# A windowed-attention and softplus feed-forward kernel: value products token by token in the scores' tile shape, softmax division on ScalarE, and visits at written times

## The chip, the cores and the metric

One core of one Trainium2 chip runs the whole program in one launch. The metric is the device time of that launch in microseconds (us), over several runs; beside it stands one execution taken by the hardware profiler, whose rows are quoted below. The engines are PE (TensorE; PEld are its weight loads), DVE (VectorE), ACT (ScalarE), POOL (GpSimd) and SP, which issues nearly all DMAs.

## What is computed

Attention of 8 heads over 4608 tokens (8 sequences of 576), head size 64, where each query sees 32 keys: the last 32 positions in heads 0 to 3, every fourth of the last 128 in heads 4 to 7. Its output, 512 features per token, goes through a feed-forward layer with softplus between its two matrices. All of it is fp32.

```python
scores = scale * np.matmul(q, k.transpose(0, 1, 3, 2))
scores = np.where(masks[None, :, :, :], scores, -1000000000.0)
attn = np.exp(scores - np.max(scores, axis=-1, keepdims=True))
attn = attn / (np.sum(attn, axis=-1, keepdims=True) + 1e-09)
x = np.matmul(attn, v)            # then tokens x 512 features
h = x @ w_in                      # 512 x 2048
g = np.maximum(h, 0.0) + np.log1p(np.exp(-np.abs(h)))
return (g @ w_out).astype(np.float32)
```

## The kernel before

**Tokens** are cut into 9 chunks of 512. A chunk's attention is four **groups** (class `Group`, L368), 36 in all; the groups of chunks 0 and 1 are called early here, those of chunks 2 to 8 late (28 of them). A group is two heads times 512 tokens: groups 0 and 1 of a chunk are the plain heads, 2 and 3 the strided ones.

**A late group** runs so: 32 small matmuls give the scores (`score`, L403: 64 contraction rows, 32 queries, 64 keys, so the array is cut into tiles of 64 rows by 32 columns). DVE scales and masks them out of PSUM (L445) and takes the maximum (L456); ACT takes eight exponentials of 64 columns each with their sums (L467); DVE takes the reciprocal of the sums (L479, L482), divides (`divide`, L485) and transposes squares of 32x32 (L507); the squares go to DRAM ("turned") and come back as `pt` with keys on the partitions (`send_squares`, `fetch_squares`). Then 32 small matmuls give the values (`weighted`, L543): the stationary operand is v (64 keys by 64 features), the moving one the weights of 32 queries, so the tiles are 64x64. The result stands feature by feature, and ACT copies it as it is out of PSUM into `x_full` (`x_high`, L592, L596), which is one kt quarter of the 512 features. Scores of one group and values of an earlier one share the bank pair `sv_ps`, each in one half of a bank.

**The feed-forward** multiplies in two or three parts (a high and a low part of each fp32 operand, tiles named `xh`/`xl`, `g` and `parts`). Chunks 0 to 2 go through it in 48 slots (`h_part` L660, `o_part` L709: each 12 matmuls of 128x512). Chunks 3 to 8 go in three pairs, each as seven products of blocks in place of eight (names a11 to s4 and t1 to t4); `prepared` (L1371) builds the sums and splits of the blocks of x from `x_full`, `product` gives h, `block_step` the output.

**What sets the order.** Up to slot 9 the order is written out by hand in `OPENING`; a word is an action and its number (S scores, M maximum, E exponentials, Pv divide, T transposes, C copy, V values, Xh and Xl the two parts of x, D decode a weight, H, G, O the feed-forward). Slots 10 to 21 follow a loop with fixed moments (`attend`, L953, for groups 8 to 11). From slot 22 on a planner writes the program: every piece of work is a `Task` with an engine, a cost and what it waits for; DVE, ACT, POOL and SP take the open task of lowest rank, PE takes from two queues of feed-forward work and from the list of **visits** (`choose`, L1898). A visit is the scores of group n, with the values of an earlier group right behind them where these are ready (`together`; for n below 20 the group before, from then on two before). A visit is due 12 or 16 us after the last (`VISIT_EVERY`, `LATE_VISITS`). The order that comes out is kept as written on each engine. All matmuls stand at L242, all DMAs of SP at L177.

Of the kernel before, what the change touches and what calls it, by code (L numbers as in the profile page):

```python
# [24 lines left out]
P = 128  # L25
# [11 lines left out]
PKW = CH + WIN  # L37
DKW = DIL * (CH // DIL + WIN)
SW = NS * WKEYS
# [15 lines left out]
PREPARED_SOONER = -3.0  # L55
# [4 lines left out]
FAMILY_SOONER = 5.0  # L60
LATE_VISITS = 16.0
# [9 lines left out]
HANDED_VISIT = 2.0  # L71
MARGIN = 0.4
VISIT_EVERY = 12.0
# [25 lines left out]
v0 S4 Dl1_0 M4 k5 C0 q5 r3 E2 T1 V0 C1 D0_0_1 v1 Pv3 Z2 Pv2 T2 D1_0_1 Xh0 v2 Xl0 E4 C2 D2_0_1 D3_0_1  # L99
D0_2_0 v3 r4 S5 M5 D4_0_1 Z4 H1_0 E5 r5 D1_2_0 D2_2_0 D3_2_0 k6 q6 H0_0 Pv4 T3 V1 r6 v4 Xh1 C3 D5_0_1 V2  # L100
Xh2 Xl1 T4 Z5 Xl2 C4 V3 r7 Xh3 D4_2_0 k7 v5 Pv5 H1_1 H1_2 D0_1_1 Xl3 H0_1 D5_2_0 D1_1_1 H1_3 D0_3_0
Dl0_1 A1 Dl2_0 H0_2 H0_3 S6 D1_3_0 D2_3_0 A0 D3_3_0 T5 C5 G1 H2_0 D2_1_1 D3_1_1 D4_3_0 D5_3_0 H2_1 G0
H2_2 H2_3 M6 Dl3_0 Gs1 Gs0 Gl0 V4 H3_0 H3_1 H3_2 D0_4_0 D0_2_1 D1_2_1 D2_2_1 Xh4 D4_1_1 Xl4 H3_3 O0_0 E6
Gl1 Z6 D5_1_1 D3_2_1 D4_2_1 Dl1_1 D1_4_0 D2_4_0 A2 O0_1 O0_2 G2 V5 Xh5 Xl5 D3_4_0 D4_4_0 A3 G3 D5_4_0
Dl4_0 O0_3 Gs2 Gl2 O1_0 O1_1 O1_2 q7 r8 D0_3_1 r9 S7 O1_3 r10 M7 r11 v6 r12 v7 D0_4_1 D5_2_1 Dl2_1 Pv6
H4_0 H4_1 H5_0 H5_1 H4_2 E7 H4_3 r13 D1_3_1 O2_0 O2_1 r14 A4 T6 D1_4_1 D2_4_1 C6 O2_2 V6 D3_4_1 Z7
D2_3_1 D3_3_1 D4_3_1 D0_5_0 G4 Pv7 O2_3 H6_0 H6_1 D5_3_1 Xh6 Gs3 Xl6 D4_4_1 D1_5_0 r15 T7 r16 m2 r17 q8
r18 H5_2 H6_2 Dl3_1 D2_5_0 Gl3 C7 Gs4 V7 r19 D0_7_0 D5_4_1 O3_0 O3_1 D1_7_0 Dl4_1 Xh7 Xl7 Gl4 H5_3
D0_6_1 O3_2 H6_3 D1_6_1 D3_5_0 D2_6_1 A5 O3_3 O4_0 O4_1 D4_5_0 D5_5_0 G5 O4_2 H7_0 D2_7_0 A6 Dl5_0
D3_7_0 D3_6_1 K0 D0_6_0 Gs5 r20 G6 H7_1 O4_3 D1_6_0 D4_6_1 H7_2 H8_0 H8_1 H8_2 D4_7_0 Gl5 D5_6_1 r21 k8  # L110
v8 r22 Gs6 D5_7_0 K1 Dl6_1 D2_6_0 Dl7_0 r23 D0_8_0 K2 D0_5_1 K3 H8_3 H7_3 O5_0 D3_6_0 Gl6 D1_8_0 O5_1
D1_5_1 D4_6_0 O5_2 r24 O5_3 A7 D5_6_0 A8 r25 D2_8_0 D2_5_1 G7 r26 r27 r28 O6_0 O6_1 O6_2 H9_0 H9_1 Gs7
H9_2 D3_5_1 D3_8_0 H9_3 D4_5_1 D4_8_0 D5_5_1 D5_8_0 Gl7 O6_3 G8 A9 O7_0 O7_1 r29 r30 Gs8 Dl8_0 Dl5_1 G9
O7_2 Gl8 Dl6_0 O7_3 Gs9 r31 Gl9
# [4 lines left out]
def tile_windowed_attention_softplus_ffn(  # L119
# [4 lines left out]
    kdl: bass.AP,  # L124
    vp: bass.AP,
# [160 lines left out]
    def load_mask(c):  # L286
# [6 lines left out]
        load_dma(out=masks[c], in_=cst[c, :, P:] if c < FIRST else msk[c])  # L293
# [42 lines left out]
    WHOLE = slice(0, 2)  # L336

    def combine(d, name, kt=WHOLE):

# [5 lines left out]
            out=raw_block(d, name)[:, kt], in0=raw_block(d, a)[:, kt], in1=raw_block(d, b)[:, kt], op=op  # L345
        ))

    def split_high(d, name, kt=WHOLE):
# [4 lines left out]
        pin(nc.scalar.copy(out=blocks[name][0][:, kt], in_=raw_block(d, name)[:, kt]))  # L353

    def split_low(d, name, kt=WHOLE):
        high, low = blocks[name]
        pin(nc.vector.tensor_tensor(
            out=low[:, kt], in0=raw_block(d, name)[:, kt], in1=high[:, kt].bitcast(F32), op=ALU.subtract
        ))

    def first_of(dil, t, g):

        t2, h = divmod(t, 2)
        if dil:
            return g * PER + (2 * h + t2) * BLK, g * (PER + WIN) + (2 * h + t2) * BLK
        return ((h * 2 + t2) * NG + g) * BLK, ((h * 2 + t2) * NG + g) * BLK
# [1688 lines left out]
```

## Time and profile before

| | before |
|---|---|
| median of 3 runs | 826.92 us (825.87 to 827.13) |
| profiled execution, first to last instruction | 827.4 us |
| PE busy | 813.3 us, 98% |
| DVE busy | 654.0 us, 79% |
| ACT busy | 579.0 us, 70% |
| POOL busy | 65.0 us, 8% |
| DMA | 194.81 MB, mean 235 GB/s |

The runs are whole executions; the profile is one execution with its rows counted from the first to the last instruction, 0.5 us above the median. In the rows, "x64" is a count of instructions put together, "[1.17 <-DVE s]" an idle time and what ended it. A fp32 matmul of the small shapes leaves two records, so the 32 matmuls of a group are x64. A record's own length is longer than the distance from one start to the next, since matmuls overlap; it is the starts that tell the pace.

### The profile page before, as it was taken

The numbers are of one execution on the slowest core, as the hardware profiler recorded it, in microseconds if no ns is written. First come the engines' busy times: TensorE is split into PE (matmuls) and PEld (weight loads), VectorE is DVE, ScalarE is ACT, GpSimd is POOL, SyncE is SP. The second block draws the span as 40 slices with busy tenths as digits, with TensorE's granted clock in tenths as the row PEclk, the third lists the DMA queues.
The fourth block names the chain that finished last, engine by engine and source line by source line (L and its number), as shares of the span: only waits on it lengthen the run. The fifth ranks groups of instructions, "written<-read, shape, count | busy, mean of one in ns | idle before, by whom it ended". The sixth has DMA issues, their size and how long they took to land.

```text
span 827.4 us, 19611 instructions
## 1 busy us (share of the span) xinstructions
PE 813.3 (98%) x7861; PEld 663.0 (80%) x7861; DVE 654.0 (79%) x936; ACT 579.0 (70%) x1241; POOL 65.0 (8%) x74
## 2 busy tenths in 40 slices
PE   7899999999999999999999999999999999999998
PEld 3778888888888888888888888888778887888886
DVE  5798899957797788787889886978899757577964
ACT  6898778757676877588878637788696345776732
POOL 0000000031354360000000000000000000000000
PEclk9899999999999999999999999999999999999999
DMA  8895934468999887756677878888766576666652
GB/s 285 290 315 179 323 95 144 135 206 281 299 311 349 302 313 239 226 147 196 219 256 256 300 238 274 296 281 268 238 208 205 190 243 203 191 203 210 221 194 88
DMA packets 102778, 194.81 MB, mean 235 GB/s; under 512 B 9248, under 2 KB 49568, under 8 KB 102688
## 3 DMA queue, kind: packets, MB, share of 16 engines
q1 hardware_dynamic: 102544, 193.29, 71.3%
q8 instruction: 62, 1.02, 0.5%
q10 hardware_dynamic: 144, 0.28, 0.1%
q14 instruction: 28, 0.23, 0.1%
HBM read 145.29 MB, written 48.23 MB: 234 GB/s over the span
## 4 chain that ended last, share of the span: by engine, by line
PE 90%; DMA 9%; ACT 0%; DVE 0%; issue 0%; DVEq 0%; SPq 0%
PE o_ps L242 43%; PE h_ps L242 14%; PE h_x L242 13%; PE h_y L242 13%; PE sv_ps L242 6%; DMA raw<-w 3%; DMA v<-vp 3%; DMA k<-kpl 1%; DMA t<-w_o 1%; DMA turned<-squares 1%; DMA pt<-turned 1%; PE a_ps L242 0%; DVE g L1499 0%; ACT g L1495 0%; ACT pt L534 0%
## 5 line engine op out<-in xcount | busy, mean ns | idle before, releaser
L242 PE MATMUL o_ps<-g,t 128*128 128x512 f32 x867 | 208.1, 389 | 0.7 <-DMA t<-w_o 0.7
L242 PEld LDWEIGHTS o_ps<-g,t 128*128 128x128 f32 x867 | 162.1, 188 | 34.8 <-DMA t<-w_o 1.2
L242 PE MATMUL o_ps<-g,parts 128*128 128x512 f32 x576 | 142.3, 392 | 0.0
L242 PE MATMUL h_ps<-xh,parts 128*128 128x512 f32 x384 | 130.2, 397 | 0.0
L242 PEld LDWEIGHTS o_ps<-g,parts 128*128 128x128 f32 x576 | 107.2, 188 | 22.4
L1495 ACT CAST g<-stored 128x1024 fp32r<-128x1024 f32 x72 | 75.5, 1050 | 66.2 <-PE o_ps L242 63.0
L1499 DVE TENSOR_TENSOR g<-stored,g 128x1024 fp32r<-128x1024 f32 x72 | 87.8, 1221 | 32.4 <-ACT g L1495 32.1
L242 PEld LDWEIGHTS h_ps<-xh,parts 128*128 128x128 f32 x384 | 72.6, 189 | 15.7
L467 ACT ACTIVATE s<-s,nm 128x64 f32<-128x64 f32 x224 | 74.9, 337 | 8.3 <-DVE nm L456 8.0
L242 PE MATMUL h_ps<-xl,parts 128*128 128x512 f32 x192 | 75.3, 392 | 0.0
L242 PE MATMUL h_x<-s,t 128*128 128x512 f32 x276 | 70.5, 391 | 0.0
L242 PE MATMUL h_y<-s,t 128*128 128x512 f32 x276 | 70.4, 390 | 0.0
L818 POOL TENSOR_TENSOR a<-a 128x256 f32<-128x256 f32 x64 | 59.1, 929 | 99.0 <-DVE a L813 86.9
L242 PEld LDWEIGHTS h_y<-s,t 128*128 128x128 f32 x276 | 51.6, 188 | 10.9
L1475 DVE SCALAR_TENSOR_TENSOR stored<-stored,e 128x1024 f32<-128x1024 f32 x48 | 58.3, 1218 | 2.5 <-ACT e L1471 2.5
L242 PEld LDWEIGHTS h_x<-s,t 128*128 128x128 f32 x276 | 51.6, 188 | 10.8
L1490 DVE TENSOR_TENSOR stored<-stored 128x1024 f32<-128x1024 f32 x48 | 58.3, 1219 | 0.4
L682 DVE SCALAR_TENSOR_TENSOR e<-h_ps,e 128x512 f32<-128x512 f32 x48 | 32.8, 683 | 25.2 <-ACT e L1170 20.5
L1465 ACT ACTIVATE e<-stored 128x1024 f32<-128x1024 f32 x48 | 50.4, 1054 | 2.4 <-DVE stored L1454 1.2
L1471 ACT ACTIVATE e<-e 128x1024 f32<-128x1024 f32 x48 | 50.8, 1060 | 1.0
L1468 ACT ACTIVATE e<-e 128x1024 f32<-128x1024 f32 x48 | 50.7, 1057 | 0.9
L467 ACT ACTIVATION_READ_ACCUMULATOR s<-s,nm 128x1 f32 x224 | 42.3, 189 | 0.0
(104 smaller groups left out, 1244.4 us busy)
## 6 DMA issues: line engine op xcount, KB each, us to landing
t<-w_o SPq DMA_DIRECT2D x84, 512.0 KB, 4.2
raw<-w SPq DMA_DIRECT2D x64, 256.0 KB, 5.2
v<-vp SPq DMA_DIRECT2D x28, 512.0 KB, 5.2
t<-w SPq DMA_DIRECT2D x20, 512.0 KB, 4.0
t<-w_two SPq DMA_DIRECT2D x20, 512.0 KB, 4.4
q<-qp SPq DMA_DIRECT2D x35, 256.0 KB, 3.7
w_o<-stage SPq DMA_DIRECT2D x32, 256.0 KB, 3.9
t<-w_one SPq DMA_DIRECT2D x16, 512.0 KB, 4.7
```

Source lines behind the costliest of these rows:

```text
L242: return tc.keep_in_program_order(nc.tensor.matmul(**kw))
L467: pin(nc.scalar.activation(out=self.blocks[:, t], in_=src, func=AF.Exp, bias=self.nm[:, t : t + 1], scale=1.0 / 8.0 if self.masked else 1. ...
L682: pin(nc.vector.scalar_tensor_tensor(out=e, in0=tiles.pop(i), scalar=0.0, in1=e, op0=ALU.max, op1=ALU.add))
L818: pin(nc.gpsimd.tensor_tensor(out=out, in0=in0, in1=in1, op=ALU.subtract))
L1465: pin(nc.scalar.activation(out=es[key], in_=raw_g(*key), func=AF.Abs))
L1468: pin(nc.scalar.activation(out=es[key], in_=es[key], func=AF.Exp, scale=-1.0))
L1471: pin(nc.scalar.activation(out=es[key], in_=es[key], func=AF.Ln, bias=1.0))
L1475: pin(nc.vector.scalar_tensor_tensor(out=h, in0=h, scalar=0.0, in1=es.pop(key), op0=ALU.max, op1=ALU.add))
L1490: pin(nc.vector.tensor_tensor(out=raw_g(c, *PLACE[name]), in0=raw_g(c, *PLACE[a]), in1=raw_g(c, *PLACE[b]), op=op))
L1495: pin(nc.scalar.copy(out=set_of(k)[0], in_=raw_g(c, *PLACE[name])))
L1499: pin(nc.vector.tensor_tensor(out=low, in0=raw_g(c, *PLACE[name]), in1=high.bitcast(F32), op=ALU.subtract))
```

## The change

**Late groups** hold four heads times 256 tokens in place of two heads times 512 (two groups for the plain heads, two for the strided). The values matmuls are swapped: the weights are stationary (64 keys by 32 queries) and v moves (64 features), so they have the scores' tile shape, 64x32, and the result stands token by token. It is not divided before: `divide` is gone for late groups, and `shares` reads the values out of PSUM with eight ACT instructions of 64 columns, each scaled by the reciprocal of its sum, back into `pt`. `unturned` then turns squares of 32x32 on DVE into `x_full` (one instruction of 512 columns for strided heads, two of 256 for plain ones). The copy L596 is gone.

**Early groups** get the same values matmuls (their division stays where it was); `unturned` turns them out of PSUM into `s`, and `x_high` and `x_low` read that and no longer PSUM. With this a kt quarter of the features of a chunk takes two groups, where before it took one.

**Loads.** A late group has its own mask (128 KB; before, one for the four groups of a chunk) and 640 columns of keys (before, 544 for plain heads).

**Order.** `VISITS_AT` gives each visit of the planner's part a written time, in place of the two spacings; the ranks of two families of tasks are moved (`FAMILY_SOONER` 5 to 13, `PREPARED_SOONER` -3 to 4); the planner's costs follow (values 1.30 to 1.00, both together 2.10 to 1.60; new: shares 1.70, unturned 0.72 or 0.84); the next `bring` waits for `unturned` of the group before and no longer for its values; `OPENING` is written anew.

```diff
-PKW = CH + WIN
+PKW = CH + 2 * WIN
+LKW = DIL * (CH // DIL + WIN)
+MW = NS // 2 * WKEYS
-PREPARED_SOONER = -3.0
+PREPARED_SOONER = 4.0
-FAMILY_SOONER = 5.0
-LATE_VISITS = 16.0
+FAMILY_SOONER = 13.0
-HANDED_VISIT = 2.0
-MARGIN = 0.4
-VISIT_EVERY = 12.0
+VISITS_AT = (
+    4, 27.5, 40, 50.5, 60, 85.5, 101, 108.5, 140, 149.5, 174, 189.5,
+    204, 211.5, 235, 250.5, 266, 281.5, 297, 304.5, 332, 343.5, 363, 378.5,
+)
+MARGIN = 0.5
...
+    def load_mask(c, pr=0):
+        if c >= FIRST:
+            masks[c, pr] = wk.tile([P, 2 * SW], BF16, name="mask", bufs=1)
+            load_dma(out=masks[c, pr], in_=msk[c - FIRST, pr])
+            return
...
         def weighted(self, shared=None, following=None):
+            if self.c >= FIRST:
+                by_block = self.v.rearrange("p i r d -> p (i r) d")
+                for m, g in itertools.product(range(NS), range(NG)):
+                    at_col = m // 2 * HALF + MW + m % 2 * D
+                    for h in range(2):
                         begun = matmul(
-                            out=dst,
-                            lhsT=self.v[h * WKEYS : (h + 1) * WKEYS, i, r, :],
-                            rhs=self.weights_of(h, r * 2 + t2, g),
+                            out=banks[h][g * SQ : (g + 1) * SQ, at_col : at_col + D],
+                            lhsT=self.weights_of(h, m, g),
+                            rhs=by_block[h * WKEYS : (h + 1) * WKEYS, m * NG + g],
...
+        def shares(self):
+            self.x = self.pt.rearrange("p g n -> p (g n)").rearrange("p (b n) -> p b n", n=D)
+            for n in range(NB):
+                m, h = n // 2, n % 2
+                at_col = m // 2 * HALF + MW + m % 2 * D
+                divided = nc.scalar.activation(
+                    out=self.x[:, n], in_=self.values_in[h][:, at_col : at_col + D], func=AF.Copy,
+                    scale=self.ri[:, n : n + 1],
+                )
+                pin(divided)
...
+        def unturned(self):
             if self.c >= FIRST:
+                by_square = self.x.rearrange("p b (d k) -> p b d k", d=2)
+                x = x_half(self.c, self.dil)
+                if self.dil:
+                    pin(nc.vector.transpose(
+                        out=x[:, :, self.j * HALF : (self.j + 1) * HALF].rearrange("p d (b q) -> p b d q", q=SQ),
+                        in_=by_square,
+                    ))
+                    return
+                for d in range(2):
+                    by_block = x[:, d].rearrange("p (c b q) -> p b c q", c=DIL, q=BLK // DIL)
+                    pin(nc.vector.transpose(
+                        out=by_block[:, self.j * NB : (self.j + 1) * NB],
+                        in_=by_square[:, :, d].rearrange("p b (c q) -> p b c q", c=DIL),
+                    ))
                 return
...
         def x_high(self):
-            for dh, _, src in self.x_parts():
-                copied = nc.scalar.copy(out=dh, in_=src)
-                pin(copied)
+            high, x = self.x_part(0)
+            pin(nc.scalar.copy(out=high, in_=x))
...
     def values_of(n):
-        v = valued[n] = Task(f"values {n}", PE, 1.30, lambda: value_of(n), deps)
+        v = valued[n] = Task(f"values {n}", PE, 1.00, lambda: value_of(n), deps)
+        shares = Task(f"shares {n}", ACT, 1.70, groups[n].shares, [v, scaled_of.get(partner(n)), divided_of.get(n)], rank=0.3)
         x_done[n] = Task(
-            f"x {n}", ACT, 0.60, groups[n].x_high, [v, scaled_of.get(partner(n)), *x_uses.get(n // 2, [])], rank=0.3
+            f"unturned {n}", DVE, 0.72 if groups[n].dil else 0.84, groups[n].unturned,
+            [shares, *x_uses.get(n // 2, [])], rank=0.3,
         )
...
-        last = Task(f"divide {n}", DVE, 0.70, lambda: g.divide(nc.vector), [last], rank=0.3)
-        brought[n] = Task(f"bring {n}", SP, 0.5, g.fetch_squares, [last, Later(lambda: valued.get(n - 1))], rank=0.1)
+        brought[n] = Task(f"bring {n}", SP, 0.5, g.fetch_squares, [last, Later(lambda: x_done.get(n - 1))], rank=0.1)
...
-        together[scored[n]] = Task(f"both {n}", PE, 2.10, both)
-    spaced, done_second = HANDED_VISIT, 0
+        together[scored[n]] = Task(f"both {n}", PE, 1.60, both)
...
-            if t >= spaced and visits[0].open(t) and (urgent or visits[1] in scores or joins(visits[1], t)):
+            visit_at = VISITS_AT[len(VISITS_AT) - sum(v in scores for v in visits)]
+            if t >= visit_at and visits[0].open(t) and (urgent or visits[1] in scores or joins(visits[1], t)):
                 return visits
...
-                spaced = t + (VISIT_EVERY if len(visits) > 32 else LATE_VISITS)
```

**Where the order moves.** PE, the visit with the scores of the last group (`sv_ps<-k,q`), before:

```order
L242 MATMUL h_y<-s_4335,t 128x512 x4
L242 MATMUL h_y<-s_4336,t 128x512 x2
L242 MATMUL sv_ps<-k,q 32x64 x32
L242 MATMUL sv_ps<-pt,v 64x4x8 x32
L242 MATMUL h_x<-a_4374,t 128x512 x4
L242 MATMUL h_x<-a_4375,t 128x512 x2
```

and of the change:

```order
L246 MATMUL h_x<-s_4564,t 128x512 x4
L246 MATMUL h_x<-s_4565,t 128x512 x2
L246 MATMUL sv_ps<-k,q 32x64 x32
L246 MATMUL sv_ps<-v,pt 32x64 x32
L246 MATMUL h_y<-a_3909,t 128x512 x4
L246 MATMUL h_y<-a_3910,t 128x512 x2
```

The same two pieces stand side by side; the values (`sv_ps<-..` the second row) have the scores' shape 32x64 now. Over the whole planner's part and the loop ahead of it, 21 of the 28 late groups had their values right behind scores; of the change it is 19. The last two groups' values, which stood 54 and 84 matmuls of 128x512 behind this visit, stand 48 and 174 behind it.

PE in the opening (`t_ps` transposes of the weights, `a_ps` values of an early group, `s_ps` scores), before:

```order
L496 MATMUL t_ps<-ident,s 128x128 x4
L242 MATMUL a_ps<-pt,v 64x4x8 x32
L496 MATMUL t_ps<-ident,s 128x128 x4
L242 MATMUL s_ps<-k,q 32x64 x32
L242 LDWEIGHTS consts
L242 MATMUL s_ps<-mask,consts 128x256
```

and of the change:

```order
L517 MATMUL t_ps<-ident,s 128x128 x4
L246 MATMUL a_ps<-v,pt 32x2x32 x32
L517 MATMUL t_ps<-ident,s 128x128 x4
L246 MATMUL a_ps<-v,pt 32x2x32 x32
L246 MATMUL s_ps<-k,q 32x64 x32
L246 LDWEIGHTS consts
```

The values of group 1 now stand ahead of the scores of group 5; before, they stood behind these and the first six matmuls of the feed-forward.

ACT near that last visit (`s,sm<-s,nm` exponentials, `e` softplus), before:

```order
L1471 ACTIVATE e<-e 128x1024
L467 ACTIVATE s,sm<-s,nm 128x64 x5
L596 COPY x_full<-sv_ps 128x512
L1495 CAST g<-stored 128x1024
L1452 COPY temps<-h_y 128x512
L353 CAST a_3928<-x_full 128x1024
```

and of the change:

```order
L1547 ACTIVATE e<-e 128x1024
L1550 ACTIVATE e<-e 128x1024
L1531 COPY temps<-h_y 128x512
L623 ACTIVATE pt<-sv_ps,ri 128x64 x8
L488 ACTIVATE s,sm<-s,nm 128x64 x3
L1531 COPY stored<-h_y 128x512
```

One copy `x_full<-sv_ps` is replaced by eight instructions `pt<-sv_ps,ri`; here they stand ahead of the last group's exponentials, where the copy stood behind them.

## Rows read from the trace of the kernel before

**Rows 1.** The page: span, part 1, and the clock of part 2

```profile
span 827.4 us, 19611 instructions
PE 813.3 (98%) x7861; PEld 663.0 (80%) x7861; DVE 654.0 (79%) x936; ACT 579.0 (70%) x1241; POOL 65.0 (8%) x74
...
PEclk9899999999999999999999999999999999999999
```

**Rows 2.** Waits of PE: waited for, us in total, times, longest

```profile
PE s_ps L242 <- issue: 3.0, 3, 1.4
...
PE sv_ps L242 <- DMA pt<-turned: 1.0, 2, 0.5
...
PE o_ps L242 <- DMA t<-w_o: 0.7, 1, 0.7
```

**Rows 3.** Timeline of PE, a joint visit: start, length, instructions

```profile
203.81 1.52 PE L242 MATMUL o_ps<-g,parts 128*128 128x512 f32 x6
205.26 0.86 PE L242 MATMUL sv_ps<-k,q 64*32 64x64 f32 x64
206.05 1.14 PE L242 MATMUL sv_ps<-pt,v 64*64 64x32 f32 x64
207.12 1.67 PE L242 MATMUL o_ps<-g,parts 128*128 128x512 f32 x6
```

**Rows 4.** Timeline of PE in 206.10 to 206.15 alone

```profile
205.89 0.23 PE L242 MATMUL sv_ps<-k,q 64*32 64x64 f32 x2
206.05 0.32 PE L242 MATMUL sv_ps<-pt,v 64*64 64x32 f32 x8
```

**Rows 5.** Groups of PE by line: busy us, mean ns, idle before

```profile
L242 PE MATMUL sv_ps<-pt,v 64*64 64x32 f32 x1792 | 32.4, 220 | 1.0 <-DMA pt<-turned 1.0
L242 PE MATMUL sv_ps<-k,q 64*32 64x64 f32 x1792 | 24.1, 224 | 0.0
```

**Rows 6.** Timeline of PE: the values of an early group

```profile
42.90 1.14 PE L242 MATMUL a_ps<-pt,v 64*64 64x32 f32 x64
43.97 0.50 PE L242 MATMUL h_ps<-xh,parts 128*128 128x512 f32 x1
```

**Rows 7.** ACT: the copy's group by line, and one exponential in the timeline

```profile
L596 ACT COPY x_full<-sv_ps 128x512 f32<-128x512 f32 x28 | 16.2, 580 | 15.6 <-DVE s L445 13.2 <-PE sv_ps L242 2.3
...
209.13 0.34 ACT L467 ACTIVATE s<-s,nm 128x64 f32<-128x64 f32 x1
209.37 0.19 ACT L467 ACTIVATION_READ_ACCUMULATOR s<-s,nm 128x1 f32 x1
209.47 0.33 ACT L467 ACTIVATE s<-s,nm 128x64 f32<-128x64 f32 x1
```

**Rows 8.** DVE by line: division, transpose, and 256 columns from PSUM

```profile
L485 DVE TENSOR_TENSOR s<-s,ri 128x512 f32<-128x512 f32 x32 | 23.6, 736 | 0.8
...
L507 DVE STREAM_TRANSPOSE squares<-s 128x512 f32<-128x512 f32 x28 | 19.8, 708 | 0.6
...
L436 DVE TENSOR_REDUCE nm<-s_ps 128x4 f32<-128x256 f32 x10 | 3.8, 419 | 2.2 <-PE s_ps L242 2.2
```

**Rows 9.** Windows: PE, PEld, DVE, ACT, POOL busy; clock, DMA share, GB/s

```profile
190.00:324.00 134.00, 134.00 (x1423) 110.05 (x1422) 107.97 (x168) 95.12 (x247) 52.07 (x56) 1.00 0.93 313
324.00:429.00 105.00, 105.00 (x1117) 85.84 (x1116) 82.84 (x114) 84.72 (x190) 0.00 (x0) 1.00 0.64 202
```

**Rows 10.** Opening: timeline of PE, then clock of 24 to 31 (PE alone)

```profile
25.95 0.78 PE L242 MATMUL h_ps<-xh,parts 128*128 128x512 f32 x1
...
24.00:31.00 7.00, 5.92 (x99) 0.51 0.90 306
```

**Rows 11.** The last joint visit: PE behind its values, its copy, bringing pt

```profile
581.29 0.50 PE L242 MATMUL h_x<-a,t 128*128 128x512 f32 x1
...
588.03 0.56 ACT L596 COPY x_full<-sv_ps 128x512 f32<-128x512 f32 x1
...
pt<-turned SPq DMA_DIRECT2D x56, 128.0 KB, 3.3
```

More of the change, by code (lines that the diff above doesn't have):

```diff
@@ L124, in tile_windowed_attention_softplus_ffn @@
     kdl: bass.AP,
+    kl: bass.AP,
     vp: bass.AP,
@@ L592, in x_high @@
-        def x_high(self):
-            if self.c >= FIRST:
-                self.x = x_half(self.c, self.pr // 2)[:, self.pr % 2], None, self.src
-            for dh, _, src in self.x_parts():
-                copied = nc.scalar.copy(out=dh, in_=src)
-                pin(copied)
-                if self.c >= FIRST and partner(self.n) < len(groups):
-                    behind_of(copied, groups[partner(self.n)].scaled_by, "one engine at a time reads a bank")
+                if following and not following.scaled_by:
+                    following.beside = begun
@@ new lines, in weighted @@
+                self.values_in = banks
+                return
+            for g, t2 in itertools.product(range(NG), range(2)):
+                i = t2 * NG + g
+                for h in range(2):
+                    for r in range(2):
+                        quad = slice((2 * t2 + r) * SQ, (2 * t2 + r + 1) * SQ)
+                        keys_of = slice(h * WKEYS, (h + 1) * WKEYS)
+                        by_square = banks[h][quad].rearrange("p (d g k) -> p d g k", d=2, k=SQ)[:, :, NG:]
+                        matmul(
+                            out=by_square[:, :, g],
+                            lhsT=self.weights_of(h, r * 2 + t2, g),
+                            rhs=self.v[keys_of, i, r, :],
+                            start=True,
+                            stop=True,
+                        )
@@ new lines, in weighted, with columns @@
+            self.src = src
+        def columns(self, a, per=CH // DIL):
+            if self.dil:
+                if per == CH // DIL:
+                    a = a[:, :, self.j * HALF : (self.j + 1) * HALF]
+                return a.rearrange("p d (h n) -> p h d n", h=2)
+            a = a.rearrange("p d (c n) -> p d c n", c=DIL)
+            if per == CH // DIL:
+                a = a[:, :, :, self.j * 2 * BLK : (self.j + 1) * 2 * BLK]
+            return a
+        def shares(self):
[6 more added lines that the diff above has]
+                    scale=self.ri[:, n : n + 1],
+                )
+                pin(divided)
+                if n == 0 and partner(self.n) < len(groups):
+                    behind_of(divided, groups[partner(self.n)].scaled_by, "one engine at a time reads a bank")
@@ L621, in load @@
             groups[n].load()
-            if groups[n].pr == 0 and groups[n].c not in masks:
-                load_mask(groups[n].c)
     def load_v(n):
@@ L775, in tile_windowed_attention_softplus_ffn @@
         "V": lambda g: groups[g].weighted(),
+        "Xt": lambda g: groups[g].unturned(),
         "Xh": lambda g: groups[g].x_high(),
@@ L1340, in attention @@
         scaled = scaled_of[n] = Task(
-            f"scaled {n}", DVE, 0.69, g.maximum, [s, turned_of.get(n - 1), masks_in.get(g.c)], rank=0.25
+            f"scaled {n}", DVE, 0.69, g.maximum, [s, turned_of.get(n - 1), masks_in.get(n)], rank=0.25
         )
@@ L2006, in _layout @@
-    late = vp[FIRST:].reshape(NCH - FIRST, NPR, 2, 2, SQ, 2, NG, 2, D)
+        for j in range(2):
+            for h in range(2):
+                for g in range(NG):
+                    s = c * CH + j * HALF + (h * NG + g) * BLK
+                    part = va[:, s : s + WKEYS].reshape(2, 2, WKEYS, D)
+                    vp[c, j, h, :, :, g] = part.transpose(2, 0, 1, 3)
+                    s = c * per + g * BLK
+                    part = vd[:, 2 * j + h, s : s + WKEYS].reshape(2, 2, WKEYS, D)
+                    vp[c, 2 + j, h, :, :, g] = part.transpose(2, 0, 1, 3)
```

270 lines of the change are left out of this document (151 added, 119 removed).

## The prediction

> **What bounds the kernel now.** I read the page first. PE is busy 813.3 us of the 827.4 us span, and the granted clock is full in all but two of the 40 slices [rows 1]. So time can only be saved by giving PE less to do, or by ending the 14.1 us in which it idles. Next the waits of PE: most of them stand before `s_ps`, that is in the opening; behind it there are only 1.0 us before values whose weights `pt` were not back from DRAM (twice 0.5) and 0.7 us before an output product [rows 2]. The rest of the 14.1 us is the start and the tail behind the last matmul. From about 35 us on, PE is the path: what is taken from PE there is won in full, as long as nothing that feeds it becomes late.
>
> Then the timeline of one joint visit [rows 3]. Six large matmuls take 1.36 us (12 of them 2.72 us, so 0.227 each); here six begin at 203.81, so the seventh would begin at 205.17. The scores begin at 205.26, the values at 206.05, the next large matmul at 207.12. So the scores hold PE for 0.79 us and the values for 1.07 us, though both are 32 matmuls. Entering costs 0.09 us, and coming back 0.15 us (the six large ones behind last 1.67 us to the end of the last, the six ahead 1.52). The groups by line show that this is so for all 28 late groups: scores 24.1 us busy, values 32.4 us, with 1792 records each, so 0.86 and 1.16 us a group when the overlap at the ends is counted in [rows 5].
>
> One row more: the last scores begin at 205.89, the first values at 206.05 [rows 4]. Inside the scores a record begins every 0.010 us (205.26 to 205.89 for 62 of them). So at the border no matmul begins for some 0.14 us longer than usual, although no idle time is shown, because earlier matmuls are still running. Borders between large matmuls of different tiles have no such hole (they keep 0.227 us from start to start).
>
> **The change on PE.**
> *Values in the scores' shape.* The same number of matmuls, with 32 stationary columns and 64 moving ones, as the scores have. No row shows values in that shape; the bounds are 1.07 us as now and 0.79 us as the scores [rows 3]. I take 0.79, the row of the same shape, tile positions in the same alternation, and the same two banks. 28 x 0.28 = **7.8 us** less.
>
> *No change of shape inside a visit.* 19 late groups have their values right behind scores. If the hole of 0.14 us comes from the change of the tile shape, it goes there: 19 x 0.14 = **2.7 us** less; if it belongs to any start behind a wait, nothing. I take the first, since large matmuls that wait show no hole. The Trainium skill, TensorEngine Tiling (Array Packing), section Key Properties, says that changing the tiling mode, not merely the tile, drains TensorE; by that rule the hole goes, and without it the sum would be 2.7 us smaller.
>
> *Early values.* Eight groups; four stand behind 40 us, each 1.07 us (42.90 to 43.97) [rows 6], so 4 x 0.28 = **1.1 us** less. The four before stand among waits and count nothing.
>
> *Visits.* Two joint visits fewer and so two visits more: 2 x (0.09 + 0.15) = **0.5 us** more.
>
> Sum on PE: -7.8 - 2.7 - 1.1 + 0.5 = **-11.1 us**.
>
> **The change beside PE.** *ACT.* The copy (0.58 us, 28 times) goes; eight instructions of 64 columns with a scale per row come. Their price is not in the trace. From below: an exponential of 64 columns is followed by the next instruction 0.24 us after its start (209.13 to 209.37); from above: with its read of the sum, 0.34 us to the next exponential (209.47) [rows 7]. These have no sum, so I take 0.24: 1.9 us a group, 1.4 us more than the copy, 28 x 1.4 = 39 us in all; from above it would be 60 us. ACT goes from 579 to about 618 us, 76% of the span. Cover: in the busiest stretch, 324 to 429 us, ACT has 84.7 of 105 us now [rows 9]; six groups there add 8 us and leave 12. On the path nothing is added as long as that is spread.
>
> *DVE.* The division (0.74 us) goes, the turn comes: 0.71 us for strided heads as L507, and two instructions of 256 columns, 0.42 us each as the nearest row of that size, for plain ones [rows 8]. That is 28 x 0 and 14 x 0.1: 1 us, nothing. The early groups get eight turns of 0.7 to 0.8 us with nothing taken away, 6 us in the first 70 us.
>
> *POOL*, 8% busy [rows 1], loses four divisions. *DMA and SP:* 21 masks more of 128 KB, and 48 KB more of keys for each of 14 plain groups (640 columns for 544), some 3.4 MB on 194.8. In 190 to 324 us, the fullest stretch, 0.93 of the DMA time is used [rows 9]; six groups add 1 MB to 42 MB, 2%. The mask of group n is asked for when group n-1 has been scaled, a visit ahead, so its wait on SP (two or three other loads queue behind it) is hidden by the 10 us and more to the next visit. Nothing.
>
> *Bringing pt.* It now waits for `unturned` of the group before, since the shares lie in `pt`, and no longer for its values only. From the values' end: scaling 0.7 us (512 columns on DVE), shares 1.9, turn 0.8, issue to landing 3.3 in the median [rows 7, 8, 11], 6.7 us with no queueing. Visits are 48 to 78 large matmuls apart where it matters (10.9 us or more), so 4.2 us are left for queueing at the tightest. The two half-microsecond waits for `pt` [rows 2] stood before the last two groups; the very last has 174 large matmuls now in place of 84, so its wait goes; I set against it one new wait of the same size. Sum 0.
>
> *The opening.* A kt quarter of x takes two groups now, so the first product waits for the values of group 1 and their turn, high part and low part (0.8 + 0.6 us on the way more). It began at 25.95 with PE at half clock (0.51 of full in 24 to 31 us, the lower level of 1.2 GHz) [rows 10]. I expect it about 1 us later; but the values of group 1 (1.3 us at that clock) are then behind it. Zero, with 1.5 us less and 2.5 us more as bounds: PE's waits decide the clock there.
>
> **Sum.** 827.4 - 11.1 = 816.3 us for the profiled execution, which stands 0.5 us above the median of 826.92. So the forecast is **815.8 us**; the bounds around it: 813 when the opening gains 1.5 us and its four early values count too (4 x 0.28), 818.5 when the holes stay.
>
> **Rivals.**
> *Waits eat a third to two thirds* (818.5 to 823 us). ACT is in order, and every shares of 1.9 us stands ahead of softplus work. For it: ACT 81% in 324 to 429 us. The Trainium skill, ScalarE: Activation LUTs, section Rules for kernel authors, says to multiply on VectorE, not ScalarE, which speaks against this part. If half of the added 1.4 us comes through to PE in the 10 visits of that stretch and the next, 7 us come back: 823. Against: PE waited for no ACT result behind the opening [rows 2] with ACT at that load. Chance 0.15.
>
> *Values no faster* (826 us). Should the pace be set by reading v or by writing 64 columns, and not by the shape, PE saves between nothing and the holes less the visits (2.2 us): 825 to 827. Against: the scores do just that at 0.79. Chance 0.05.
>
> *Slower: pt comes late for every group from 20 on.* These 16 have their values two visits behind their scores, and `pt` can be brought only when the group before is turned. The last joint visit shows how late ACT can be: PE left the values at 581.29, the copy began at 588.03 [rows 11], 6.7 us on. If the shares begin as late: 6.7 + 1.9 + 0.8 + 3.3 = 12.7 us, against 10.9 us to the next values where the visits are closest (48 large matmuls), a wait of 1.8 us, and 13.0 us (54 of them and the scores ahead), no wait yet, at the more usual distance. It decides from 11.1 / 16 = 0.7 us a group; at 1.0 us, which takes shares or landings 1.3 us later still, the time is 832. For it: the chain has a step on ACT and one on DVE more. Against: most visits are 54 large matmuls or more apart, and the listing has the shares ahead of the exponentials. Chance 0.07.
>
> **How the numbers follow.** Forecast and its own bounds (813 to 818.5): 0.63. Waits: 0.15. No faster: 0.05. Slower: 0.07. Opening better than 813: 0.06; between 823 and 825: 0.04. The range 813 to 822.5 leaves about 0.2 out. About 0.2%, 1.6 us, is what a measurement can tell from no change: faster 0.88 (0.63 + 0.15 + 0.06 + 0.04), same 0.05, slower 0.07.
>
> **What would show it.** Right: values and scores of a joint visit begin 0.65 us apart, and the next large matmul 0.79 us behind the values; the 1792 value records busy about 24 us; ACT near 618 us, DVE within 8 us of 654; PE busy about 802 us, its waits behind the opening under 3 us in all. Wrong: rows of PE waiting for `pt`, for ACT `g` or `e`, or for `t` that sum to more than 3 us; a value group still at 1.07; the first product of the feed-forward later than 28 us or the half clock lasting beyond 33 us.

## The result, and the profile after

The changed kernel takes **830.73 us** (median of 5 runs, 829.30 to 832.80), the kernel before 826.92 us (5 runs, 823.79 to 827.75): a ratio of 1.0059, 95% interval 1.0039 to 1.0080. It is slower; 815.8 us was forecast. A run's time is 1.8 us more than its span, so the profiled execution of before (span 827.4) is one of 829.2 us, 2.3 above its median (not 0.5, as the prediction had it; its forecast, 826.92 - 11.1, is the same by either); that of after (span 831.0) is one of 832.8. Between the two profiles there are +3.6 us to explain.

The page of after, for [rows 1]:

```profile
span 831.0 us, 19932 instructions
PE 804.5 (97%) x7861; PEld 648.8 (78%) x7861; DVE 655.4 (79%) x966; ACT 607.6 (73%) x1436; POOL 57.6 (7%) x70
...
PEclk9799999999999999999999999999999999999999
```

PE is busy 8.8 us less, and idle 26.5 us in place of 14.1. So the work went as intended, and 12.4 us of new waiting took its place. First what was won: a joint visit of after (timeline of PE), for [rows 3], and the groups by line, for [rows 5]. Of the 19 joint visits, 15 are like this one; in the other four the values begin 0.67 to 0.77 us behind the scores, in place of 0.66.

```profile
254.88 0.86 PE L246 MATMUL sv_ps<-k,q 64*32 64x64 f32 x64
255.54 0.85 PE L246 MATMUL sv_ps<-v,pt 64*32 64x64 f32 x64
256.32 0.97 PE L246 MATMUL o_ps<-g,parts 128*128 128x512 f32 x3
```

```profile
L246 PE MATMUL sv_ps<-v,pt 64*32 64x64 f32 x1792 | 24.4, 225 | 2.2 <-issue 1.4 <-PE h_y L246 0.5 <-DMA pt<-turned 0.4
L246 PE MATMUL sv_ps<-k,q 64*32 64x64 f32 x1792 | 24.1, 224 | 0.0
```

The values hold PE for 0.78 us, as the scores do; 1792 records are busy 24.4 us, 8.0 less. Now the waits of PE (us in total, times, longest), for [rows 2]:

```profile
PE h_ps L246 <- DVE e L757: 2.2, 2, 1.2
PE a_ps L246 <- issue: 2.2, 1, 2.2
...
PE h_ps L246 <- ACT xh L676: 1.6, 2, 1.2
PE o_ps L246 <- ACT s L488: 1.6, 2, 1.4
...
PE sv_ps L246 <- issue: 1.4, 1, 1.4
...
PE h_y L246 <- issue: 1.0, 1, 1.0
PE h_ps L246 <- ACT parts L237: 0.9, 1, 0.9
...
PE h_ps L246 <- DVE xl L680: 0.9, 2, 0.6
PE h_x L246 <- DVE e L757: 0.8, 1, 0.8
...
PE sv_ps L246 <- DMA pt<-turned: 0.4, 1, 0.4
```

Before, PE waited for no result of ACT or DVE behind 33 us; here is a list of such waits, and two more in the late part (`sv_ps` and `h_y` behind "issue") end with nothing that the profile shows. Where the waits lie, the windows tell (columns as in [rows 9]); of before, then of after:

```profile
20.00:40.00 20.00, 17.43 (x435) 14.13 (x433) 15.59 (x37) 16.21 (x61) 0.00 (x0) 0.83 0.88 285
40.00:100.00 60.00, 59.95 (x624) 48.65 (x623) 53.80 (x102) 49.84 (x123) 0.00 (x0) 1.00 0.82 273
300.00:450.00 150.00, 150.00 (x1622) 122.71 (x1621) 123.42 (x168) 121.01 (x260) 7.91 (x8) 1.00 0.70 227
```

```profile
20.00:40.00 20.00, 14.32 (x352) 10.13 (x353) 15.16 (x37) 13.26 (x52) 0.00 (x0) 0.74 0.93 322
40.00:100.00 60.00, 55.47 (x601) 42.15 (x601) 51.00 (x100) 46.14 (x105) 0.00 (x0) 1.00 0.65 214
300.00:450.00 150.00, 146.83 (x1724) 118.12 (x1723) 123.12 (x174) 126.50 (x317) 11.42 (x13) 1.00 0.78 257
```

Idle time of PE grew by 3.1 us in 20 to 40, by 4.5 in 40 to 100 and by 3.2 in 300 to 450. A second measure parts the opening from the rest: the start of the first late scores, ahead of which PE does the same 222 large matmuls in every kernel here (instructions on `sv_ps`; before, after, and e1 of the next section):

```profile
L242 PE MATMUL sv_ps<-k,q x1792: 212/216/240, 92.4 to 580.0; 64*32 64x64 f32 x200
L246 PE MATMUL sv_ps<-k,q x1792: 212/216/242, 101.1 to 593.8; 64*32 64x64 f32 x200
L246 PE MATMUL sv_ps<-k,q x1792: 212/216/242, 90.9 to 582.7; 64*32 64x64 f32 x200
```

Up to there the change takes 8.7 us more than the kernel before, and from there to the end 5.1 us less (729.9 against 735.0).

ACT did not become fuller in the opening but emptier: 13.3 of 20 us, where it had 16.2. It stands still, and this piece shows for what (timeline of all engines of after in 48 to 52, rows of ACT, DVE and PE):

```profile
48.26 0.78 DVE L661 STREAM_TRANSPOSE s<-a_ps 128x256 f32<-128x256 f32 x2
...
49.06 0.62 ACT L676 CAST xh<-s 128x512 fp32r<-128x512 f32 x1 [1.65 <-DVE s L661]
...
49.72 0.69 DVE L680 TENSOR_TENSOR xl<-s,xh 128x512 fp32r<-128x512 f32 x1
...
50.45 0.31 ACT L488 ACTIVATE s<-s_ps,nm 128x64 f32<-128x64 f32 x1 [0.76 <-DVE xl L680]
...
51.79 0.50 PE L246 MATMUL o_ps<-g,parts 128*128 128x512 f32 x1 [1.39 <-ACT s L488]
```

ACT has nothing to do with the turn, but its next instruction, the high part of x, reads what DVE turns. DVE comes to the turn late, because decoding stands ahead of it, and part of that waits for ACT in its turn. Behind the high part wait the exponentials of a later group, which must leave the banks o1 and o2, and for those PE waits 1.39 us. The group of that line adds it up: in front of seven of its eight `xh` ACT stood still, 9.6 us in all, for the turn (before: 3.0, and for PE).

```profile
L676 ACT CAST xh<-s 128x512 fp32r<-128x512 f32 x8 | 4.9, 618 | 9.6 <-DVE s L661 6.2 <-DVE s L655 3.4
```

### The profile page after: what moved, and what is told of

Read it like the earlier page. It is cut to its first block, busy times and chain, and to the rows that moved or that the text cites. A ratio compares the mean times of both kernels' runs of the same rounds, so it can differ in the third digit from the quotient of the medians.

```text
span 831.0 us, 19932 instructions
## 1 busy us (share of the span) xinstructions
PE 804.5 (97%) x7861; PEld 648.8 (78%) x7861; DVE 655.4 (79%) x966; ACT 607.6 (73%) x1436; POOL 57.6 (7%) x70
## 5 line engine op out<-in xcount | busy, mean ns | idle before, releaser
L246 PE MATMUL o_ps<-g,parts 128*128 128x512 f32 x576 | 144.1, 393 | 2.1 <-ACT s L488 1.6
L894 POOL TENSOR_TENSOR a<-a 128x256 f32<-128x256 f32 x64 | 56.6, 892 | 258.6 <-DVE a L889 239.6
L246 PEld LDWEIGHTS h_x<-s,t 128*128 128x128 f32 x276 | 51.6, 188 | 11.1 <-issue 0.2
L623 ACT ACTIVATE pt<-sv_ps,ri 128x64 f32<-128x64 f32 x224 | 48.7, 331 | 10.4 <-DVE s L465 7.7
```

The lines of the kernel that those rows point to most:

```text
L246: return tc.keep_in_program_order(nc.tensor.matmul(**kw))
L623: divided = nc.scalar.activation(out=self.x[:, n], in_=self.values_in[h][:, at_col : at_col + D], func=AF.Copy, scale=self.ri[:, n : n + 1],)
L894: pin(nc.gpsimd.tensor_tensor(out=out, in0=in0, in1=in1, op=ALU.subtract))
```

## The experiments

The theory from this reading: the late part does roughly what was forecast (in fact about half to two thirds of it, as will be seen), and the **early turn** gives it back, less by its own 6 us of DVE than by two engines waiting for each other in order. Rivals: the late part lost it (shares on ACT, written times); the opening's new order lost it (two groups for a quarter of x). Each kernel ran beside the kernel before, whose median was 825.5 to 826.6 us in these. In e1, e2, e3 and e5 the features of the first two chunks are out of order: these four do the work, but not the whole computation.

| kernel | us | ratio to before (95%) |
|---|---|---|
| the change | 830.73 | 1.0059 (1.0039 to 1.0080) |
| e1 late part alone | 820.85 | 0.9939 (0.9923 to 0.9955) |
| e2 no early turn | 821.29 | 0.9943 (0.9926 to 0.9959) |
| e3 turn, order of before | 827.79 | 1.0007 (0.9991 to 1.0022) |
| e5 turn out of the chain | 823.72 | 0.9978 (0.9967 to 0.9989) |
| e6 turn done by PE | 831.42 | 1.0068 (1.0048 to 1.0087) |
| e9 turn into pt | 830.35 | 1.0047 (1.0030 to 1.0064) |
| e8 queues reordered | 827.88 | 1.0024 (1.0008 to 1.0039) |
| e12 one step more | 825.64 | 0.9993 (0.9979 to 1.0007) |
| e11 groups 2, 3 first | 828.73 | 1.0031 (1.0015 to 1.0047) |
| e13 group 3 first | **823.97** | 0.9977 (0.9956 to 0.9998) |
| e4 old planner rules | 844.02 | 1.0213 (1.0196 to 1.0230) |
| e7 division on DVE | 840.27 | 1.0176 (1.0153 to 1.0200) |
| e10 preparation at -3 | 830.04 | 1.0044 (1.0027 to 1.0061) |
| e14 preparation at 2 | 828.92 | 1.0021 (1.0005 to 1.0036) |

**Which half?** e1 puts the early groups and `OPENING` of before into the changed kernel.

```diff
-            for g, t2 in itertools.product(range(NG), range(2)):
...
+            for i in range(NB):
+                t2, g = divmod(i, NG)
...
+                            lhsT=self.v[h * WKEYS : (h + 1) * WKEYS, i, r, :],
+                            rhs=self.weights_of(h, r * 2 + t2, g),
```

> The changed kernel with the early groups (0 to 7) as they were before: the opening's table, the values with the weights moving, no turn on VectorE, one quarter of x for each group; the late groups and the planner as changed. (What the first two chunks compute is not the reference's.) Theory 'the loss lies in the opening': TensorE's extra idle time in the first 100 us of the changed kernel, 16.8 against 8.6 us, goes, and the early values' gain of 1.1 us with it: 830.7 - 8.2 + 1.1 = 823.6, between 821 and 825, and TensorE's idle in the first 100 us is back at 8 to 10 us. Rival 'the late part lost it' (visits, shares on ScalarE): 829 or more, with idle in the late part grown.

Measured 820.85 us. The windows of e1:

```profile
20.00:40.00 20.00, 17.36 (x460) 14.07 (x461) 17.75 (x42) 18.66 (x71) 0.00 (x0) 1.00 0.97 329
40.00:100.00 60.00, 59.95 (x623) 48.60 (x622) 53.30 (x103) 49.83 (x124) 0.00 (x0) 1.00 0.81 270
300.00:450.00 150.00, 147.12 (x1724) 118.39 (x1723) 124.58 (x172) 127.25 (x308) 8.26 (x8) 1.00 0.78 253
```

The opening's idle time is gone, that of 300 to 450 is not. So the new opening costs 9.9 us (830.73 - 820.85). The late part alone is a gain of 5.5 by the medians. The two profiles differ by 8.3 (819.1 against 827.4), but 1.5 of that lies ahead of the first late scores (90.9 against 92.4), where both kernels do the same; behind them it is 6.8. By either figure it is less than the 10.0 of the sum without the early values.

**Turn or order?** e2 leaves the turn out (the split reads the banks) and keeps the new order; e3 keeps the turn and takes the old order, with a quarter of x for each group.

```diff
-Pv3 Z2 Pv2 T2 Xt0 D1_0_1 Xh0 v2 Xl0 V1 E4 Xt1 Xh1 C2
+Pv3 Z2 Pv2 T2 D1_0_1 Xh0 v2 Xl0 V1 E4 Xh1 C2
...
-            pin(nc.scalar.copy(out=high, in_=x))
+            for dst, src in self.x_parts(0):
+                pin(nc.scalar.copy(out=dst, in_=src))
```

> The changed kernel without the turn of the early groups on VectorE: the copy and the subtraction that split x read the values' banks, as before the change, and the eight STREAM_TRANSPOSE steps are left out; the new order of the opening and the two groups that a quarter of x waits for stay. (The features of the first two chunks are then out of order.) Theory 'the turn is the cost' (6 us of VectorE work ahead of the split, between the values and the first products): 823 to 826. Rival 'the order is the cost' (a quarter needs two groups): 829 to 831. If both share: 826 to 829.

> The changed kernel, turn kept, but with the opening's order of before (the turn of each group put right ahead of its split) and with each group's split written to a quarter of x of its own, so that a product waits for one group and not for two. (The features of the first two chunks are then out of order.) Theory 'the turn is the cost': 829 to 832. Rival 'the order is the cost': 823 to 825.

Without the turn, the order costs next to nothing (821.29 against 820.85; what the swapped early values win is in it). With it, 6.9 us are lost in the old order and 9.4 in the new. So the two groups that a quarter needs cost little by themselves; the step that I had counted at nothing costs nearly all. Both ranges for the turn were a little too high: e2 lies 1.7 us below its 823, e3 1.2 below its 829.

**Its load or its place?** e5 is e2 (x is split from the banks) with transposes of the same size where the turns stood, for which nobody waits.

```diff
+            for half in HALVES:
+                if not self.dil:
+                    pin(nc.vector.transpose(out=self.s[:, half], in_=self.s[:, half]))
+            if self.dil:
+                pin(nc.vector.transpose(out=self.s, in_=self.s))
```

> The kernel without the early turn, but with transposes of the same size standing on VectorE where the turns stood: from the finished weights' tile into itself, so that no split of x waits for them and they wait for nothing late. (The features of the first two chunks are out of order, as without the turn.) It tells the load of the turn from its place in the chain. Theory 'load' (VectorE is 80 to 98% busy in the opening, 6 us more of work delay all that follows): 827 to 831. Rival 'chain' (the split, and ScalarE's queue behind it, wait for VectorE's turn): 821 to 823.

823.72 us, just above what the chain alone gives: the load is 2.4 us (823.72 - 821.29), the place in the chain the other 7.0 (830.73 - 823.72); by the ratios 2.9 and 6.7. In e5 ACT stood still 0.2 us ahead of its `xh`, in the changed kernel 9.6. The first late scores say the same: they begin at 92.4 us in e2, 94.3 in e5 and 101.1 in the change.

**Can PE do the turn?** e6 has the weights moving again, 32 features at a time, so that the features come out where the new layout wants them. A group then takes 64 matmuls in place of 32 (the 128 and 64 of the expectation count records).

```diff
-                            lhsT=self.weights_of(h, r * 2 + t2, g),
-                            rhs=self.v[keys_of, i, r, :],
+                                lhsT=self.v[h * WKEYS : (h + 1) * WKEYS, i, r, d * SQ : (d + 1) * SQ],
+                                rhs=self.weights_of(h, r * 2 + t2, g),
```

> The whole computation without an early turn: the values of groups 0 to 7 with the weights moving again, but with 32 features of a head at a time standing (128 matmuls 64x32 with 32 columns instead of 64 with 64), so that the features come out in the new order in the banks and the split reads them there. It does what the change does, by TensorE instead of VectorE. If the turn is what costs, this comes near the kernel without the turn (821.3) plus the doubled values, 8 x 0.6 to 0.9 us = 5 to 7 us at most and less where TensorE waits anyway: 822 to 827. If the turn is not the cause: 830.

831.42 us: a miss, and not by the matmuls' own length. Group by line of PE:

```profile
L246 PE MATMUL a_ps<-pt,v 64*32 64x32 f32 x1024 | 12.1, 209 | 10.1 <-issue 8.7 <-DVE xl L695 0.9 <-ACT s L488 0.4
```

They are busy 4.7 us more than the changed kernel's 7.4, and 8.7 us more PE waits for nothing that the profile shows, in the middle of a row of matmuls, five times and up to 3.2 us. Some such time stands in every opening here (3.0 us before, [rows 2]); in 20 to 40 us, where four of the five lie, the DMA engines are 0.93 busy. What PE lacked there was not tested. The change has one such stop too, 2.24 us in the middle of group 1's values (25.56 us), ahead of the first product. It is not what was lost: e9, below, has the same order without it and takes 830.35.

**Can order give it back?** e9 turns into the tile `pt` instead of `s`, which frees the exponentials from the wait at 50.45; e8 does that and rearranges `OPENING` in eight places (two of them below); e12 moves one step more.

```diff
-            self.x = self.s.rearrange("p (d n) -> p d n", d=2)
+            self.x = self.pt.rearrange("p (d n) -> p d n", d=2)
```

```diff
-Xt0 D1_0_1 Xh0 v2 Xl0 V1 E4 Xt1 Xh1 C2 D2_0_1 Xl1 D3_0_1
+Xt0 D1_0_1 v2 V1 E4 Xh0 Xl0 D2_0_1 D3_0_1 Xt1 C2 Xh1 Xl1
...
-Xt4 Xh4 D4_1_1 Xl4 H3_3 O0_0 E6 Gl1 Z6
+Xt4 D4_1_1 H3_3 O0_0 E6 Xh4 Gl1 Z6 Xl4
```

> The changed kernel, one line different: the early turn writes into the tile of the turned weights (pt), which the values have just read, and not into the tile s, so that the next group's exponentials need not wait until the split of x has been read out of s (in the changed kernel's profile the exponentials at 50.45 us start 0.76 us after ScalarE is free, behind VectorE's xl, and two o_ps products wait 1.6 us for them). The order in each queue stays. Theory 'queues' (ScalarE waits in order for the turn): 829 to 831, since the exponentials still stand behind the split in ScalarE's queue. Rival 'the tile s is held too long': 826 to 828.

> As the one before, and with the opening's table rearranged where ScalarE or VectorE stood still for the turn: in eight places the split (or the turn) stands behind work that was ready (group 0's split behind group 2's exponentials, group 4's behind group 6's, group 5's behind the next slot's activation, the turns of groups 1, 2 and 6 behind decoding or a softplus); nothing is added or left out. Theory 'chain in the queues' (7 of the turn's 9.5 us are waits in order): 3 to 6 us come back, 824.5 to 828. Rival 'load or data': 829 to 831.

e9 gives nothing, as the queue theory says: the exponentials still stand behind the split. e8 gives 2.8 us. Its first product waited, though, and DVE's timeline shows for what:

```profile
28.95 0.80 PE L246 MATMUL h_ps<-xh,parts 128*128 128x512 f32 x1 [2.23 <-ACT xh L676]
```

```profile
25.74 0.69 DVE L680 TENSOR_TENSOR xl<-pt,xh 128x512 fp32r<-128x512 f32 x1 [1.77 <-ACT xh L676]
```

I had made the same fault the other way round: DVE stood in front of group 0's low part, and the turn of group 1 behind it. e12 swaps these two.

```diff
-E4 Xh0 Xl0 D2_0_1 D3_0_1 Xt1 C2 Xh1 Xl1
+E4 Xh0 D2_0_1 D3_0_1 Xt1 C2 Xh1 Xl0 Xl1
```

> As e8_reordered, with one step moved: the subtraction of group 0 (xl) stands behind the turn of group 1 in VectorE's queue, where in e8_reordered VectorE stood still 1.77 us for it and group 1's turn, and with it the first product, waited behind (first product at 28.95 us, 2.23 us of wait). Theory 'queues': the first product comes at 26.5 to 27.5 us and 1 to 2 us of e8_reordered's 827.9 go: 825.5 to 827. Rival (the first product is held by the data, not by the place): 827.5 to 828.5.

825.64 us, the first product at 27.02. Nothing was added or left out against the change, and 5 us have come back. Two runs went on from there. e11 puts the chains of groups 2 and 3 ahead of group 5's scores. e13, shown here, puts the turn of group 3's weights and its copy ahead of group 5's exponentials, and its values, turn and split ahead of group 2's values; unlike what its expectation says, these three still stand behind group 5's exponentials.

```diff
-S5 M5 D4_0_1 Z4 H1_0 E5 r5 D1_2_0 D2_2_0 D3_2_0 k6 q6 H0_0 Pv4 T3 H1_1 r6 v4 C3 D5_0_1 D0_1_1 V2
+S5 T3 M5 D4_0_1 Z4 C3 H1_0 E5 r5 D1_2_0 D2_2_0 D3_2_0 k6 q6 H0_0 Pv4 V3 H1_1 r6 v4 Xt3 Xh3 D5_0_1 D0_1_1 V2
```

> As e12_repair, and the chains of groups 2 and 3 (turn of the weights, values, turn of x, split) put ahead of group 5's scores and exponentials, so that the third and fourth quarter of x stand ready when the first products are done (e8_reordered waits 1.33 us for them at 37.8). Nothing is added or left out. Theory 'queues': another 1 to 2 us, 824 to 826, under the kernel before. Rival: group 5's later exponentials hold the o banks and cost as much: 826 to 829.

> As e12_repair, with group 3's chain (turn of the weights, copy, values, turn of x, split) put ahead of group 5's exponentials and group 2's values, group 5's exponentials otherwise where they were. e12_repair's third quarter of x waits 1.38 us for group 3's split at 35.7 us. Theory 'queues': 0.8 to 1.4 us of that go: 824.2 to 825 (not more, since group 2's values still wait for group 5's exponentials to leave the o banks). Rival: ScalarE's activations come later in turn, as in e11_early_values: 826 or more.

e11 loses 3 us against e12: the exponentials of group 5 begin at 36.4 us, the first activation of a product behind them at 41.4 (37.9 in e12), and PE waits 3.4 us for the `e` that hangs on it. e13 is **823.97 us**, 2.6 us under the kernel before beside it (by the ratio 1.9, interval 0.2 to 3.6) and 6.8 under the change, with all of the computation done. Its wait for the third quarter is still there (1.72 us); the product behind it begins at 34.82 us, where it was 35.66.

**The late part.** e4 has the old spacing of the visits and the three old constants, e7 the division on DVE ahead of the turn with one plain copy on ACT, e10 and e14 the preparation's constant alone (e10 on e8, e14 on e12).

```diff
-            if t >= visit_at and visits[0].open(t) and (urgent or visits[1] in scores or joins(visits[1], t)):
+            if t >= spaced and visits[0].open(t) and (urgent or visits[1] in scores or joins(visits[1], t)):
```

```diff
+        last = Task(f"divide {n}", DVE, 0.70, lambda: g.divide(nc.vector), [last], rank=0.3)
-        shares = Task(f"shares {n}", ACT, 1.70, groups[n].shares, [v, scaled_of.get(partner(n)), divided_of.get(n)], rank=0.3)
+        shares = Task(f"shares {n}", ACT, 0.60, groups[n].shares, [v, scaled_of.get(partner(n))], rank=0.3)
```

```diff
-PREPARED_SOONER = 4.0
+PREPARED_SOONER = 2.0
```

> The changed kernel with the planner's old rule for the visits (12 apart, then 16, the first at 2) and its old constants (family 5, prepared -3, margin 0.4); all else as changed. If the written times and the new constants are worth something: 833 to 838, with more waits of TensorE in the planner's part than the 3.8 us of the changed kernel. If they cost what is lost there: 827 to 829. If they are neutral: 830 to 832.

> The changed kernel with the late groups' weights divided by VectorE ahead of the turn again (in groups 8 to 10 by GpSimd, as before the change), and the values taken from the banks by one copy on ScalarE instead of eight scaled ones; all else as changed. VectorE then does 25 x 0.7 = 18 us more, ScalarE 28 x 1.2 = 34 us less. If ScalarE's longer shares (1.75 us a group and the wait ahead of them) cost the late part: 826 to 829. If VectorE is the tighter engine there (its waits stand at 300 to 325 us): 833 or more. If neither: 830 to 832.

> As e8_reordered, with the planner's constant for the preparation of the pairs put back from 4 to -3 (so that the splits and sums of x for the products come later in VectorE's queue than the softplus and g of the slots). It asks about the 2.9 us of waits for VectorE's e and g at 300 to 325 us. If the preparation's place there is their cause, they go and the run is 1.5 to 3 us under e8_reordered; if the products then wait for the preparation, it is the same or up to 6 us over.

> As e12_repair, with the planner's constant for the preparation of the pairs at 2 instead of 4 (at -3 e10_prepared lost 2.2 us). It asks whether the 2.2 us of waits for VectorE at 306 to 330 us are an accident of the order there. If so they go without a new wait: 823.5 to 825. If VectorE is simply full there (its busy share is 97% or more from 306 to 330), another wait takes their place: 825.5 to 828.

e4 takes 13.3 us more than the change, 6 more than its range: the written times (with their constants) are worth that. e4 also tells what closed the hole between scores and values. It has the old spacing, and in 10 of its 17 joint visits that can be read apart the values begin 0.66 us behind the scores as well, so this does not hang on the written times (timeline of PE):

```profile
375.21 0.86 PE L249 MATMUL sv_ps<-k,q 64*32 64x64 f32 x64
375.87 0.85 PE L249 MATMUL sv_ps<-v,pt 64*32 64x64 f32 x64
```

e7 takes 9.5 us more than the change, so of these two versions the one that takes 0.7 us a group from DVE and gives ACT 1.0 is the better. Why is not shown: the planner made another order from e7's costs, and at 300 to 350 us, where PE is idle 8.8 us (2.2 in the change), e7's DVE is busy 39.5 of 50 us (43.5 in the change).

What did the late part lose, then? In the change PE waits 5.5 us behind 100 us (1.7 before): 2.2 for DVE's `e` and `g`, 2.4 with no releaser shown (at 401 and 557 us), 0.9 ahead of values. The waits for DVE stand at 312, 333 and 335 us (in e1 too: 1.2 for `e`, 0.8 for `e`, 0.2 for `g`). DVE's busy time (third figure) around the last two is this:

```profile
330.00:340.00 10.00, 8.95 (x99) 6.79 (x98) 9.96 (x13) 6.93 (x12) 0.00 (x0) 1.00 1.00 353
```

DVE has no room there: the preparation of x stands in its queue ahead of `e`. At 312 us it is another matter (timelines of after, DVE, ACT and PE):

```profile
306.46 0.35 ACT L488 ACTIVATE s<-s,nm 128x64 f32<-128x64 f32 x1 [0.78 <-DVE nm L477]
...
309.26 0.71 DVE L528 STREAM_TRANSPOSE squares<-s 128x512 f32<-128x512 f32 x1 [0.88 <-ACT s L488]
309.64 0.59 ACT L1243 ACTIVATE e<-h_ps 128x512 f32<-128x512 f32 x1
...
311.81 0.50 PE L246 MATMUL h_ps<-xh,parts 128*128 128x512 f32 x1 [1.16 <-DVE e L757]
```

DVE stands still 0.88 us here, because ACT is at a late group's eight exponentials (306.46 to 309.13); the product's `e` stands behind them in ACT's queue and begins at 309.64. So this wait, half of the 2.2 us, comes by way of ACT.

e10 and e14 bear this out. With either value the two waits of the preparation go (in e12 they stand at 327 and 330 us), the one behind the exponentials stays (1.2 and 1.1 us), and a new one comes at about 440 us, 3.0 and 4.4 us. This is e14's:

```profile
PE o_ps L246 <- ACT g L1574: 4.4, 1, 4.4
```

e10 takes 2.2 us more than e8, e14 3.3 more than e12 (2.3 by the ratios, and 0.9 above its range). A version without any of these waits was not found.

## Why the prediction was wrong

*Values in the scores' shape, -7.8 us:* right (0.78 us a group; 8.0 us of busy time). *The hole at the border, -2.7:* right. Values begin 0.66 us behind the scores in 15 of 19 joint visits, in place of 0.79 [rows 3], and e4 shows it with the old spacing too. This fits the rule that the prediction cites from the Trainium skill (TensorEngine Tiling (Array Packing), section Key Properties), that a change of the tiling mode drains TensorE. Behind the first late scores e1 takes 8.8 us of PE's busy time, against the -10.0 of the sum without the early values (-7.8 - 2.7 + 0.5). (The whole of e1 has 11.1 less, but 2.3 of these lie in the opening, whose instructions are the same and which ran longer at half clock in the profile of before.) *Early values, -1.1:* they are busy 7.4 us where it was 9.4, but among the opening's waits nothing of it is seen in the time.

*ACT, +39 us, not on the path:* too high by 10 (607.6 - 579.0 = 28.6), since eight shares take 1.60 us to the start of the next instruction, 0.20 each. That none of it reaches the path was not quite so (the wait at 312 us), but e7, which takes the shares' length away, is slower. By the Trainium skill, ScalarE: Activation LUTs, section Rules for kernel authors, the multiplication belongs on VectorE; e7, which has it there, is 9.5 us slower, in an order of its own. *Bringing pt, 0:* right (0.4 to 0.9 us of waits, 1.0 before), and with it the rival that was slower by pt fell: slower it was, by another mechanism.

*DVE: "the early groups get eight turns of 0.7 to 0.8 us with nothing taken away, 6 us in the first 70 us"*, counted at nothing, **is the step that failed**. I named no work that hid them in the opening, though DVE was busy 15.6 of 20 and 53.8 of 60 us there. The runs showed 9.4 us in its place (830.73 - 821.29). The load is 2.4 us (e5 - e2). The rest, 7.0 us (830.73 - 823.72), is that a step on DVE was put between PE's values and ACT's split, in queues that run in order: ACT waited 9.6 us ahead of seven instructions, and everything behind them with it. *The opening, 0, between -1.5 and +2.5:* I followed the delay of the first product alone (it came at 27.82, 1.9 later; I said about 1) and took that for the whole. It measured +9.9 with the early values in it (the change against e1); and in e9 the first product came at 26.25, 0.3 later than before, with the time at 830.35. Of the signs named for "wrong", the half clock beyond 33 us showed (0.56 of full in 32 to 34) and the first product just missed its 28. PE's waits, for which "right" had under 3 us behind the opening, came to 5.5 behind 100 us.

*The late part* fell short too. Of the 14.9 us between forecast and time, 11.0 lie in the opening (9.9 lost where 1.1 was to be won) and 3.9 in the late part (820.85 in e1, where the sum without the early values is 815.8 + 1.1 = 816.9). Of its 10.0 us, 5.5 by the medians and 6.8 by the profiles came. That is the rival "waits eat a third to two thirds", which had 0.15, on this part of the sum. It named ACT, behind whose queue about half of the 2.2 us of waits for DVE stand; DVE without room makes the other half. In e1 2.9 us of idle time show in 300 to 450 us, 0.7 of it with no releaser; what makes up the rest of the shortfall stays open.

## What to carry to other kernels

A step moved onto another engine is costed by who stands behind it in every queue, not by its length: 6 us of transposes that fit into idle time by the sum cost 9.4, mostly because ACT stood still in order for seven of the eight. When such a step comes in, move each waiting instruction behind work that is ready and look at the first idle time of each engine again; five of those 9.4 us came back with nothing left out (only places in the queues and the tile that the turn writes changed), and the repairs showed the next waits. And ask of an engine that is 90% busy in a stretch what an added instruction there delays, even where the average over the span is 79%.

## What was not expected of the hardware

Rows of many small matmuls can stop with no wait shown: with 64 of them a group in place of 32, in an opening where the DMA engines are 0.93 busy, PE stood still for 8.7 us (e6); what it lacked is open. And a long wait can cost more than itself. In e4 PE was idle for 4.58 us at 336 to 341 us; the ten large matmuls behind it took 4.63 us (ten of them take 2.43 at 79.94 us of the changed kernel), and the granted clock was 0.50 in 341 to 345 us, the lower level of 1.2 GHz:

```profile
330.00:336.00 6.00, 6.00 (x88) 1.00 0.23 90
336.00:341.00 5.00, 0.42 (x3) 0.81 0.90 329
341.00:345.00 4.00, 4.00 (x10) 0.50 0.49 176
```

(Columns: PE busy, granted clock, DMA share, GB/s.) In the opening the half clock does not fall the same way each time: e1 has the opening of before instruction by instruction, and ran 22 to 36 us at full clock, where the profile of before has 24 to 31 at half [rows 10]. Differences of a microsecond or two in the opening between single profiles are of that kind, which is why the verdicts above go by medians.
